# Attention and soft mixture of experts on one core: in blocks 2 and 3 the subtraction of k on GpSimd goes in halves behind the subtraction of q, and ScalarE casts q ahead of k

## The chip, the cores and the metric

The kernel runs on one core of one Trainium2 chip. The time is that of one execution on the device in microseconds (us), measured over several runs; a profile is one further execution, with a record of every instruction. TensorE (PE, with its weight loads shown as PEld), VectorE (DVE), ScalarE (ACT) and GpSimd (POOL) compute; the sync engine's queue (SP) issues nearly all the transfers.

## The reference, cut to what matters

```python
# q, k, v: (8, 12, 448, 64)
scores = 0.125 * q @ k.T            # causal mask, each of 96 heads
attn = exp(scores - rowmax) / (rowsum + 1e-9)
x = (attn @ v) as (3584, 768)
logits = x @ phi                    # phi: (768, 32)
slot_input = softmax_over_tokens(logits).T @ x
slot_out = per expert: relu(slot_input @ w1[e]) @ w2[e]     # 8 experts, 768 -> 1024 -> 768
out = softmax_over_slots(logits) @ slot_out
```

All arrays are float32.

## The kernel before, in words

The 96 heads are taken as 48 pairs, and `block(p)` works on pair p: heads a = 2p and a + 1. It is a software pipeline written out by hand, and each engine keeps the program's order. While block p finishes the softmax of pair p and multiplies by v, it already computes the first part of the scores of pair p + 1 (heads a + 2 and a + 3), subtracts for pairs p + 1 and p + 2, casts q of pair p + 2 and k of pair p + 3, and loads pairs p + 3 and p + 4. So "block 2" and "block 3" are the third and fourth pair.

The products are formed from float32 split in two: a rounded part in the type fp32r, and the rest.

- `cast_k` and `cast_q` (ScalarE) round raw k and q into the tiles `ks` and `qd`. There are two `ks` tiles, used by pairs in turn, but one `qd`.
- `sub_k` and `sub_q` (GpSimd, `TENSOR_TENSOR`) write the rests: that of k into the lower half of `ks`, that of q into the lower half of `r2`. A pair has 2 x 448 columns, and `slice(0, 1)` and `slice(1, 2)`, called h0 and h1, are its two heads. `sub_q` of the next pair has to wait until the matmuls of `scores2` have read the old `r2`, and `cast_q` has to wait until `sub_q` has read the old `qd`.
- `scores1_all(i)` (TensorE) adds the mask and multiplies `ks` by `qd` for head i. It is named s<-qd,ks in the profile; its first weight load has 66 columns.
- `max_keys`, `max_row` (VectorE and a transpose on TensorE) find maxima of blocks of queries: the small tile `mr`, one for each head.
- `max_spread(i)` (GpSimd, `AFFINE_SELECT`) spreads `mr` of head i into the upper rows of `r2`, as 14 x 448.
- `scores2(i)` (TensorE, s<-r,k in the profile) multiplies `r2` by a second copy of rounded k, `k2`, on top of the first scores: it adds the product with the rest of q and takes off the maximum. It needs both `sub_q` and the spread.
- `exps` (ScalarE, pt<-s) takes the exponential, and `attv_pair` (TensorE, po<-va,pt) multiplies by v. `norm`, `xtrans` and `xcopy` bring the result into x; in blocks with p odd, `logits_a` adds 8 calls of four small products to TensorE.

In block p, TensorE runs `scores2(a)`, `scores1_all(a + 2)`, `scores2(a + 1)`, `scores1_all(a + 3)`, `attv_pair(p)`, a transpose for `max_row`, in some blocks logits, `xtrans`. GpSimd runs, in blocks from 2 on, `sub_k(p + 2)`, `sub_q(p + 1)`, spread of head a + 2, spread of head a + 3. Block 1 has its own order there: q of head 0, k of head 0, q of head 1, two spreads, then k of head 1 at the block's end.

A load is issued on SP behind the subtraction that frees its buffer: `load_qk(p + 4, 1)` (raw k) behind `sub_k(p + 2)`, `load_qk(p + 3, 0)` (raw q) behind `sub_q(p + 1)`. There are two raw buffers each. SP is one queue and keeps its order, so a load that waits holds those behind it.

All engine calls go through one helper, so the profile gives them all line 67; they are told apart by tiles.

Of the kernel before, what the change touches and what calls it, by code (L numbers as in the profile page):

```python
# [82 lines left out]
def attention_soft_moe(ctx: ExitStack, tc: tile.TileContext, qk, va, phi, w, out):  # L83
# [43 lines left out]
    def load_qk(p, a, hs=slice(0, 2), eng=nc.sync):  # L127
        if p < NPAIR:
            if hs.start == 0:

                st["raw", a, p] = (qk0[:, WN * 2 * a:WN * 2 * a + 2 * S].rearrange("p (h s) -> p h s", h=2)
                                   if (p, a) in ((1, 0), (2, 1)) else
                                   kraw[p % 2 if p > 1 else 1 - p] if a else qraw[p % 2 if p else 1])
            eng.dma_start(out=st["raw", a, p][:, hs], in_=qk[p, :, a, hs])

    def loads_v(p, eng=nc.sync):
        if p < NPAIR:
            eng.dma_start(out=va_[p % 2], in_=va[p])
# [30 lines left out]
    def load_w(n):  # L169
        if n < len(order):  # L170
            t = wtiles[order[n]] = slot(n, f"w{n}")
            q, g, c = place(n), (n + 2) // 4, WN * ((n + 2) % 4)
            if n < RES or n == NBUF or q >= RES + LATE2:
                nc.sync.dma_start(out=t, in_=w[g, :, c:c + WN])
            elif 4 <= q < RES and n > NBUF:
                if q % 4 == 3:
                    nc.sync.dma_start(out=group(n), in_=w[g])
            elif n % 2:
                t = group(n)
                nc.sync.dma_start(out=t[:, 2 * WN:] if q < RES else t, in_=w[g, :, c - WN:c + WN])  # L180
# [51 lines left out]
    def kv(p):  # L232
        return heads(ks_[p % NR])[:, :, 0:S]

    def cast_q(p, hs=slice(0, 2)):
        if p < NPAIR:
            nc.scalar.activation(out=qd[:, hs], in_=st["raw", 0, p][:, hs], func=AF.Copy)

    def cast_k(p, hs=slice(0, 2)):
        if p < NPAIR:  # L240
            nc.scalar.activation(out=kv(p)[:, hs], in_=st["raw", 1, p][:, hs], func=AF.Copy)

    def sub_k(p, hs=slice(0, 2), eng=None):
        if p < NPAIR:
            ks = kv(p)[64:P, hs]
            (eng or nc.gpsimd).tensor_tensor(out=ks, in0=st["raw", 1, p][64:P, hs], in1=ks, op=ALU.subtract)
# [6 lines left out]
    def sub_q(p, hs=slice(0, 2), eng=None):  # L253
        if p < NPAIR:
            (eng or nc.gpsimd).tensor_tensor(out=r2[64:P, hs], in0=st["raw", 0, p][64:P, hs],
                                             in1=qd[64:P, hs], op=ALU.subtract)
# [67 lines left out]
    def max_spread(i):  # L324
        if i >= NHD:
            return
        p, h = divmod(i, 2)
        mr = st.pop(("mr", i))

        nc.gpsimd.affine_select(out=r2[0:NQB, h].rearrange("p (b t)->p b t", t=32),  # L330
                                in_=mr.unsqueeze(1).to_broadcast([NQB, NQB, 32]),
                                compare_op=ALU.is_equal, fill=0.0, base=0,
                                pattern=[[-1, NQB], [0, 32]], channel_multiplier=1)

    def scores2(i, cs):
        if i >= NHD:
            return
        p, h = divmod(i, 2)
        s = st["s", i]
        k2 = k2_  # L340
        for c in cs:
            o, w, m = KS * h + P * c, S - CQ0[c], min(P, KS - P * c)
            nc.tensor.matmul(s[0:m, SCOL[c]:SCOL[c] + w], k2[:, o:o + m],
                             r2[:, h, CQ0[c]:S], start=False, stop=True, skip_group_check=True)
# [60 lines left out]
    def norm(p, k):  # L405
        if k == 0:
            sm = st["sm", p] = moe.tile([P, NQ], F32, tag="sm", name=f"sm{p}", bufs=2)
            nc.vector.tensor_scalar(out=sm, in0=po2[:, :, HD], scalar1=EPS, scalar2=None, op0=ALU.add)
        elif k == 1:
            nc.vector.reciprocal(out=st["sm", p], in_=st["sm", p])  # L410
        else:
            x, sm = x_of(p), st.pop(("sm", p))
            m = NCH - 1
            nc.vector.tensor_tensor(out=x[:, 0:m].rearrange("p c (h d)->p h c d", h=2),
                                    in0=po2[:, 0:2 * m, 0:HD].rearrange("p (h c) d->p h c d", h=2),
                                    in1=sm[:, 0:2 * m].rearrange("p (h c)->p h c", h=2).unsqueeze(3)
                                    .to_broadcast([P, 2, m, HD]), op=ALU.mult)
            for h in range(2):
                a = AW * h
                nc.vector.tensor_scalar(out=x[0:AW, m, HD * h:HD * h + HD], in0=po2[a:a + AW, 2 * m, 0:HD],  # L420
                                        scalar1=sm[a:a + AW, 2 * m:2 * m + 1], scalar2=None, op0=ALU.mult)
# [95 lines left out]
    h0, h1 = slice(0, 1), slice(1, 2)  # L517
# [52 lines left out]
    def block(p):  # L570
        a, b = 2 * p, p // 6 - 1
        m6 = p % 6
        if p + 1 < NPAIR:
            loads_v(p + 1, nc.sync if p + 1 < NPAIR - 1 else nc.scalar)
        if p % 2 and p < 44 or p in (16, 30):
            load_w(st["w"])
            st["w"] += 1

        if p:
            norm(p - 1, 2)  # L580
        scores2(a, range(NCH))
        exps(a)
        if p == 0:
            copy_k2(0, h1)
            cast_q(1, h1)
            warm(START[3], pob)
            max_row(1, 0)
            max_row(1, 1)
            max_spread(1)
            sub_k(1, h1, nc.vector)  # L590
        elif p > 1:
            xcopy(p - 2)
        scores1_all(a + 2)
        if p == 0:
            warm(START[2], pob)
        for k in range(3):
            max_keys(a + 2, k)
        if p == 0:
            cast_k(2, h0)
        scores2(a + 1, range(NCH))  # L600
        exps(a + 1)
        if p == 0:
            cast_k(2, h1)
        scores1_all(a + 3)
        if m6 == 2 and p > 6:
            logits_b(b)
        max_keys(a + 3, 0)
        late_k = p == 1
        if p == 1:
            sub_q(2, h0)  # L610
            sub_k(3, h0)
            sub_q(2, h1)
            load_qk(4, 0)
        elif p:
            sub_k(p + 2, h0 if late_k else slice(0, 2))
            if not late_k:
                load_qk(p + 4, 1)
            sub_q(p + 1)
            load_qk(p + 3, 0)
        else:  # L620
            sub_q(1, h0)
            sub_q(1, h1)
            load_qk(3, 0)
            sub_k(2, h0)
        copy_k2(p + 1)
        if m6 == 2 and p > 6:
            logits_d(b, lt)
        if p:
            cast_k(p + 3)
            cast_q(p + 2)  # L630
        else:
            cast_q(2)
            cast_k(3)
        if m6 == 3 and p > 6:
            logits_al(b)
        elif m6 == 4 and p > 6:
            logits_n(b)
        attv_pair(p)
        max_row(a + 2, 1)
        max_spread(a + 2)  # L640
        if p == 0:
            sub_k(2, h1)
            load_qk(4, 1)
        for k in (1, 2):
            max_keys(a + 3, k)
        for k in range(2):
            norm(p, k)

        m = s_[(a + 1) % 3]
        parts = []  # L650
        if m6 in (1, 3, 5) and p > 1:
            j = (m6 + 3) % 6
            logits_a(b if m6 == 1 else p // 6, (j, j + 1), m[:, 0:P])
        elif m6 == 2 and p > 6:
            logits_e(b, m, 0)
        if m6 == 3 and p > 6:
            parts = [(b, 0, slice(0, P), 512)]
        elif m6 == 4 and p > 6:
            parts = [(b, 0, slice(P, 3 * P), 512)]
        elif m6 == 0 and p > 6:  # L660
            parts = [(b - 1, 1, slice(0, 3 * P), 0)]
        for d, hf, sl, o in parts:
            dispatch_a(d, hf, m[:, o:o + sl.stop - sl.start], sl)
        max_row(a + 3, 0, to=m[:, 1024 - P:1024])
        max_row(a + 3, 1)
        if m6 == 2 and p > 6:
            logits_e(b, m, 1)
        max_spread(a + 3)
        if late_k:
            sub_k(p + 2, h1)  # L670
            load_qk(p + 4, 1)
        if m6 in (1, 3, 5) and p > 1:
            logits_t(j, m[:, 0:P])
        for d, hf, sl, o in parts:
            dispatch_b(d, hf, m[:, o:o + sl.stop - sl.start], sl)
        if p:
            xtrans(p - 1)
# [8 lines left out]
    i, b, p = NHD - 1, NB - 1, NPAIR - 1  # L686
# [319 lines left out]
```

## Time and profile before

| what | before |
|---|---|
| median of three runs | 396.44 us (396.0 to 397.08) |
| the profiled execution, its own time | 395.86 us |
| its span, first to last instruction | 394.1 us |
| mean granted TensorE clock | 0.987 |
| PE busy | 365.4 us (93%) |
| PEld busy | 293.3 us (74%) |
| DVE busy | 294.9 us (75%) |
| ACT busy | 283.0 us (72%) |
| POOL busy | 256.6 us (65%) |
| load of raw k, 448 KB, median from issue to landing | 4.3 us |

The busy shares are means over the whole span. In the timeline rows used below the columns are the start in us from the span's start, the duration in us, the engine, the source line, the operation, the tile written and the tiles read, the shapes and the count; in square brackets stands the engine's idle time before the row and what ended it. In the chain of waits, which follows the last instruction back to what released it, the columns are start, duration and what.

### The profile page before, as it was taken

The numbers are of one execution on the slowest core, as the hardware profiler recorded it, in microseconds if no ns is written. First come the engines' busy times: TensorE is split into PE (matmuls) and PEld (weight loads), VectorE is DVE, ScalarE is ACT, GpSimd is POOL, SyncE is SP. The second block draws the span as 40 slices with busy tenths as digits, with TensorE's granted clock in tenths as the row PEclk, the third lists the DMA queues.
The fourth block names the chain that finished last, engine by engine and source line by source line (L and its number), as shares of the span: only waits on it lengthen the run. The fifth ranks groups of instructions, "written<-read, shape, count | busy, mean of one in ns | idle before, by whom it ended". The sixth has DMA issues, their size and how long they took to land.

```text
span 394.1 us, 14000 instructions
## 1 busy us (share of the span) xinstructions
PE 365.4 (93%) x5766; PEld 293.3 (74%) x5766; DVE 294.9 (75%) x835; ACT 283.0 (72%) x397; POOL 256.6 (65%) x214
## 2 busy tenths in 40 slices
PE   7899999999999999999999999999999998997840
PEld 3689889888988998898889888988986544533420
DVE  7787889888888888898888988888885575433540
ACT  5888889888898898888988989888864011432430
POOL 5998889888898888898988988889861000000000
PEclk9999999999999999999999999999999999999995
DMA  7858887778898788787987876887579999999997
GB/s 259 306 194 283 293 285 247 254 256 276 286 312 275 239 276 284 254 248 266 318 308 235 307 238 244 279 283 258 176 250 374 414 438 425 429 423 415 430 433 324
DMA packets 28720, 119.17 MB, mean 302 GB/s; under 512 B 3440, under 2 KB 3952, under 8 KB 26480
## 3 DMA queue, kind: packets, MB, share of 16 engines
q1 hardware_dynamic: 28512, 118.01, 82.9%
q8 instruction: 45, 0.74, 0.7%
q10 hardware_dynamic: 144, 0.27, 0.2%
q14 instruction: 19, 0.16, 0.1%
HBM read 107.25 MB, written 11.01 MB: 300 GB/s over the span
## 4 chain that ended last, share of the span: by engine, by line
PE 64%; DMA 11%; POOL 9%; DVE 6%; ACT 4%; issue 2%; SPq 0%; POOLq 0%; DVEq 0%; ACTq 0%
PE s L67 35%; PE po L67 20%; DMA w<-in_w_dram 9%; POOL r L67 6%; PE xm L67 4%; POOL ks L67 3%; DVE lm L67 2%; PE rt L67 2%; DMA kraw<-in_qk_dram 2%; DVE lg L67 1%; ACT qd L67 1%; PE pp L67 1%; PE e L67 1%; DVE si L67 1%; ACT w L67 1%
## 5 line engine op out<-in xcount | busy, mean ns | idle before, releaser
L67 DVE TRANSPOSE_TENSOR_REDUCE r<-s 128x32 f32<-128x1024 f32 x96 | 119.5, 1245 | 7.4 <-PE s L67 4.7
L67 ACT ACTIVATE pt<-s 128x1024 f32<-128x1024 f32 x96 | 98.7, 1029 | 30.8 <-PE s L67 22.5
L67 PEld LDWEIGHTS po<-va,pt 128*64 128x64 f32 x3040 | 103.6, 138 | 12.0 <-issue 11.5
L67 PE MATMUL po<-va,pt 128*64 128x65 f32 x3040 | 110.6, 224 | 0.0
L67 POOL TENSOR_TENSOR r<-qraw,qd 64x896 fp32r<-64x896 f32 (+1 forms) x49 | 99.3, 2027 | 3.2 <-ACT qd L67 1.8
L67 POOL TENSOR_TENSOR ks<-kraw,ks 64x896 fp32r<-64x896 f32 (+1 forms) x48 | 89.7, 1870 | 4.1 <-ACT ks L67 0.4
L67 POOL TENSOR_SCALAR_AFFINE_SELECT r<-mr 14x448 fp32r<-14x448 f32 x96 | 61.8, 644 | 31.9 <-DVE mr L67 27.2
L67 PE MATMUL s<-qd,ks 128*66 128x64 f32 (+3 forms) x384 | 80.2, 320 | 0.0
L67 PE MATMUL s<-r,k 128*128 128x448 f32 (+3 forms) x384 | 65.1, 291 | 3.1 <-POOL r L67 3.1
L67 PEld LDWEIGHTS s<-r,k 128*128 128x128 f32 (+1 forms) x384 | 59.3, 175 | 8.8 <-POOL r L67 6.6
L67 PEld LDWEIGHTS s<-qd,ks 128*128 128x128 f32 (+1 forms) x384 | 52.1, 182 | 2.0 <-issue 0.9
L67 ACT ACTIVATE ks<-kraw 128x896 fp32r<-128x896 f32 (+1 forms) x49 | 45.0, 920 | 5.3 <-DMA kraw<-in_qk_dram 4.1
L67 ACT ACTIVATE k<-ks 64x896 fp32r<-64x896 f32 (+1 forms) x49 | 45.8, 935 | 1.2
L67 ACT ACTIVATE qd<-qraw 128x896 fp32r<-128x896 f32 (+1 forms) x48 | 44.7, 931 | 1.3 <-POOL r L67 0.7
L67 PE MATMUL s<-tri,identb 128*128 128x192 bf16 x192 | 39.2, 268 | 0.6
L67 DVE TENSOR_REDUCE r<-r 128x16 f32<-128x32 f32 x192 | 33.7, 176 | 5.0
L67 DVE TENSOR_REDUCE mr<-s 14x32 f32<-14x128 f32 x47 | 13.1, 279 | 21.9 <-ACT qd L67 14.1
L67 PE MATMUL xm<-ident,x 128*128 128x128 f32 x188 | 28.3, 273 | 0.0
L67 ACT ACTIVATE xts<-xm 128x512 f32<-128x512 f32 x46 | 27.1, 590 | 0.0
L67 DVE TENSOR_SCALAR x<-po,sm 64x64 f32<-64x64 f32 x94 | 26.0, 276 | 0.7
L67 DVE TENSOR_TENSOR x<-po,sm 128x384 f32<-128x384 f32 x47 | 25.2, 537 | 0.0
L67 DVE COPY w<-pp 128x384 f32<-128x384 f32 x28 | 14.4, 553 | 13.2 <-PE pp L67 13.1
(148 smaller groups left out, 393.6 us busy)
## 6 DMA issues: line engine op xcount, KB each, us to landing
w<-in_w_dram SPq DMA_DIRECT2D x34, 768.0 KB, 6.6
kraw<-in_qk_dram SPq DMA_DIRECT2D x46, 448.0 KB, 4.3
qraw<-in_qk_dram SPq DMA_DIRECT2D x46, 448.0 KB, 4.5
w<-in_w_dram SPq DMA_DIRECT2D x5, 3072.0 KB, 23.9
va<-in_va_dram SPq DMA_DIRECT2D x47, 260.0 KB, 4.9
out_dram<-w SPq DMA_DIRECT2D x7, 1536.0 KB, 13.3
w<-in_w_dram SPq DMA_DIRECT2D x5, 1536.0 KB, 9.9
qk<-in_qk_dram SPq DMA_DIRECT2D x2, 448.0 KB, 7.2
```

The costliest lines, as they stand in the source:

```text
L67: return self._tc.keep_in_program_order(op(*args, **kwargs))
```

## The change

Three places of `block(p)` change, for p = 2 and p = 3 alone. GpSimd takes the whole subtraction of q first, then the spread of head a + 2, then k of head 0, the spread of head a + 3, and k of head 1. ScalarE casts q ahead of k. The loads move with the subtractions behind which they stand.

```diff
-        late_k = p == 1
         if p == 1:
             sub_q(2, h0)
             sub_k(3, h0)
             sub_q(2, h1)
             load_qk(4, 0)
+        elif p in (2, 3):
+            sub_q(p + 1)
+            load_qk(p + 3, 0)
         elif p:
-            sub_k(p + 2, h0 if late_k else slice(0, 2))
-            if not late_k:
-                load_qk(p + 4, 1)
+            sub_k(p + 2)
+            load_qk(p + 4, 1)
             sub_q(p + 1)
             load_qk(p + 3, 0)
...
-        if p:
+        if p in (2, 3):
+            cast_q(p + 2)
+            cast_k(p + 3)
+        elif p:
             cast_k(p + 3)
             cast_q(p + 2)
...
         max_spread(a + 2)
+        if p in (2, 3):
+            sub_k(p + 2, h0)
...
         max_spread(a + 3)
-        if late_k:
+        if 1 <= p <= 3:
             sub_k(p + 2, h1)
             load_qk(p + 4, 1)
```

GpSimd, from the last subtraction of block 1 into block 4, before. `mr6` to `mr11` are the maxima of heads 6 to 11; `ks0` holds pairs 4 and 6, `ks1` pairs 3 and 5.

```order
L67 TENSOR_TENSOR ks1_87<-kraw1_83,ks1_87 64x448
L67 TENSOR_TENSOR ks0_85<-kraw0_82,ks0_85 64x2x448
L67 TENSOR_TENSOR r2_93<-qraw1_88,qd_86 64x896
L67 AFFINE_SELECT r2_93<-mr6_474 14x448
L67 AFFINE_SELECT r2_93<-mr7_483 14x448
L67 TENSOR_TENSOR ks1_87<-kraw1_83,ks1_87 64x2x448
L67 TENSOR_TENSOR r2_93<-qraw0_84,qd_86 64x896
L67 AFFINE_SELECT r2_93<-mr8_565 14x448
L67 AFFINE_SELECT r2_93<-mr9_582 14x448
L67 TENSOR_TENSOR ks0_85<-kraw0_82,ks0_85 64x2x448
L67 TENSOR_TENSOR r2_93<-qraw1_88,qd_86 64x896
L67 AFFINE_SELECT r2_93<-mr10_664 14x448
```

Now, from the first instruction of block 2 (behind the same `ks1` half) to the subtraction of q in block 4:

```order
L67 TENSOR_TENSOR r2_93<-qraw1_88,qd_86 64x896
L67 AFFINE_SELECT r2_93<-mr6_472 14x448
L67 TENSOR_TENSOR ks0_85<-kraw0_82,ks0_85 64x448
L67 AFFINE_SELECT r2_93<-mr7_482 14x448
L67 TENSOR_TENSOR ks0_85<-kraw0_82,ks0_85 64x448
L67 TENSOR_TENSOR r2_93<-qraw0_84,qd_86 64x896
L67 AFFINE_SELECT r2_93<-mr8_564 14x448
L67 TENSOR_TENSOR ks1_87<-kraw1_83,ks1_87 64x448
L67 AFFINE_SELECT r2_93<-mr9_582 14x448
L67 TENSOR_TENSOR ks1_87<-kraw1_83,ks1_87 64x448
L67 TENSOR_TENSOR ks0_85<-kraw0_82,ks0_85 64x2x448
L67 TENSOR_TENSOR r2_93<-qraw1_88,qd_86 64x896
```

The whole subtraction of k in front of each block has become two halves, one on each side of the second spread; block 4 has its old order again, and its whole subtraction of k stands right behind the last half of block 3.

ScalarE in blocks 3 and 4, before and now, from the copy into `k2` in block 3 to the two casts of block 4 (`pt` are the exponentials, `xts` the copy of x):

```order
L67 ACTIVATE k2_92<-ks0_85 64x2x448
L67 ACTIVATE ks0_85<-kraw0_82 128x2x448
L67 ACTIVATE qd_86<-qraw1_88 128x896
L67 ACTIVATE pt0_94<-s2_81 128x1024
L67 ACTIVATE xts2_600<-xm2_586 128x512
L67 ACTIVATE pt1_95<-s0_79 128x1024
L67 ACTIVATE k2_92<-ks1_87 64x2x448
L67 ACTIVATE ks1_87<-kraw1_83 128x2x448
L67 ACTIVATE qd_86<-qraw0_84 128x896
```

```order
L67 ACTIVATE k2_92<-ks0_85 64x2x448
L67 ACTIVATE qd_86<-qraw1_88 128x896
L67 ACTIVATE ks0_85<-kraw0_82 128x2x448
L67 ACTIVATE pt0_94<-s2_81 128x1024
L67 ACTIVATE xts2_602<-xm2_588 128x512
L67 ACTIVATE pt1_95<-s0_79 128x1024
L67 ACTIVATE k2_92<-ks1_87 64x2x448
L67 ACTIVATE ks1_87<-kraw1_83 128x2x448
L67 ACTIVATE qd_86<-qraw0_84 128x896
```

The casts have changed places in block 3 (and likewise in block 2), while in block 4 k is still cast ahead of q.

SP, the loads of blocks 2 to 4, before and now (`kraw0` and `kraw1` here are raw k of pairs 6 and 7, then 8; `qraw1` and `qraw0` raw q of pairs 5 and 6):

```order
L67 DMA kraw0_82<-in_qk_dram 128x896
L67 DMA qraw1_88<-in_qk_dram 128x896
L67 DMA va0_89<-in_va_dram 128x520
L67 DMA w0_310<-in_w_dram 128x1536
L67 DMA kraw1_83<-in_qk_dram 128x896
L67 DMA qraw0_84<-in_qk_dram 128x896
L67 DMA va1_96<-in_va_dram 128x520
L67 DMA kraw0_82<-in_qk_dram 128x896
```

```order
L67 DMA qraw1_88<-in_qk_dram 128x896
L67 DMA kraw0_82<-in_qk_dram 128x896
L67 DMA va0_89<-in_va_dram 128x520
L67 DMA w0_310<-in_w_dram 128x1536
L67 DMA qraw0_84<-in_qk_dram 128x896
L67 DMA kraw1_83<-in_qk_dram 128x896
L67 DMA va1_96<-in_va_dram 128x520
L67 DMA kraw0_82<-in_qk_dram 128x896
```

In both blocks raw q is loaded ahead of raw k, and raw k waits for the second half of its subtraction.

## The prediction

> **What bounds the kernel now.** I read the chain of waits first. In the early blocks it runs over GpSimd, and it ends in the stream of weights behind the attention part (start, duration, what):
>
> ```profile
> 24.58 1.90 POOL ks L67
> 26.48 1.93 POOL r L67
> ...
> 332.03 35.70 DMA w<-in_w_dram
> ```
>
> The place of the change is therefore on the path that sets the end, and the question is only how much earlier or later TensorE leaves it. The second view is the timeline of weight loads on TensorE in blocks 2 to 4. Block 3 starts at 29.30 with `scores2` of head 6, block 5 at 41.04 with that of head 10:
>
> ```profile
> 27.66 0.47 PEld L67 LDWEIGHTS xm<-ident,x 128*128 128x128 f32 x4
> 29.30 0.60 PEld L67 LDWEIGHTS s<-r,k 128*128 128x128 f32 x4 [1.17 <-POOL r L67]
> ...
> 29.88 0.15 PEld L67 LDWEIGHTS s<-qd,ks 128*66 128x66 f32 x1
> ...
> 31.15 0.14 PEld L67 LDWEIGHTS s<-qd,ks 128*66 128x66 f32 x1
> ...
> 31.95 0.78 PEld L67 LDWEIGHTS po<-va,pt 128*64 128x64 f32 x24 [0.25 <-issue]
> ...
> 41.04 0.60 PEld L67 LDWEIGHTS s<-r,k 128*128 128x128 f32 x4 [0.44 <-POOL r L67]
> ```
>
> TensorE waits 1.17 us for the spread of head 6 and 0.44 us for that of head 10. These are the two waits the edit can touch. The third view is GpSimd over the same stretch:
>
> ```profile
> 23.61 2.88 POOL L67 TENSOR_TENSOR ks<-kraw,ks 64x448 fp32r<-64x448 f32 x2
> 26.43 2.10 POOL L67 TENSOR_TENSOR r<-qraw,qd 64x896 fp32r<-64x896 f32 x1
> 28.60 1.25 POOL L67 TENSOR_SCALAR_AFFINE_SELECT r<-mr 14x448 fp32r<-14x448 f32 x2
> 29.93 1.94 POOL L67 TENSOR_TENSOR ks<-kraw,ks 64x896 fp32r<-64x896 f32 x1
> 31.83 2.11 POOL L67 TENSOR_TENSOR r<-qraw,qd 64x896 fp32r<-64x896 f32 x1
> 34.01 0.64 POOL L67 TENSOR_SCALAR_AFFINE_SELECT r<-mr 14x448 fp32r<-14x448 f32 x1
> 35.54 0.64 POOL L67 TENSOR_SCALAR_AFFINE_SELECT r<-mr 14x448 fp32r<-14x448 f32 x1 [0.90 <-DVE mr L67]
> 36.26 1.94 POOL L67 TENSOR_TENSOR ks<-kraw,ks 64x896 fp32r<-64x896 f32 x1
> 38.17 2.10 POOL L67 TENSOR_TENSOR r<-qraw,qd 64x896 fp32r<-64x896 f32 x1
> 40.34 1.25 POOL L67 TENSOR_SCALAR_AFFINE_SELECT r<-mr 14x448 fp32r<-14x448 f32 x2
> ```
>
> From 23.61 to 41.6 GpSimd stands still once (gaps under 0.1 us aside), for 0.90 us, waiting for the maxima of head 9. Everywhere else it goes from one instruction to the next. So in these blocks it is GpSimd's amount of work that sets the pace, and changing its order can win no more than that 0.90 us, less whatever new idle time and new work it brings.
>
> **The change, part by part.** I follow GpSimd through the new order. Its gaps are read from the rows above: 0.07 us from a subtraction to a spread (33.94 to 34.01), 0.08 us from a spread to a subtraction, 1.91 us from start to start behind a whole k (36.26 to 38.17), and 0.06 us from the end of a spread (28.60 + 0.64 = 29.24) to TensorE's load at 29.30. A half of k has two prices, from the groups of GpSimd by shape around 19.6 (head 0 of pair 3) and around 23.6 us (head 1 of the same pair):
>
> ```profile
> L67 POOL TENSOR_TENSOR ks<-kraw,ks 64x448 fp32r<-64x448 f32 x1 | 1.2, 1151 | 0.0
> L67 POOL TENSOR_TENSOR ks<-kraw,ks 64x448 fp32r<-64x448 f32 x1 | 1.0, 975 | 0.1
> ```
>
> I take 1.15 for the first half and 0.975 for the second: 2.13 us instead of 1.94, so 0.19 more in each of the two blocks. The lower bound is 0.975 for each. [...]
>
> The maxima come from VectorE, in these rows:
>
> ```profile
> 26.87 0.24 DVE L67 TENSOR_REDUCE mr<-rt 14x32 f32<-14x128 f32 x1
> ...
> 32.39 1.24 DVE L67 TRANSPOSE_TENSOR_REDUCE r<-s 128x32 f32<-128x1024 f32 x1
> 33.55 0.24 DVE L67 TENSOR_REDUCE mr<-rt 14x32 f32<-14x128 f32 x1
> ...
> 35.20 0.28 DVE L67 TENSOR_REDUCE mr<-s 14x32 f32<-14x128 f32 x1 [0.51 <-PE s L67]
> ```
>
> *Block 2.* The half from block 1 ends at 23.61 + 0.975 = 24.59. The whole q starts there and ends at 26.69, 1.84 earlier than before (28.53). The spread of head 6 now waits for VectorE: 26.87 + 0.24 + 0.06 = 27.17, so GpSimd idles 0.4 us that it did not idle before; it ends at 27.81. First half of k: 27.89 to 29.04. Spread of head 7: 29.11 to 29.75. Second half: 29.83 to 30.80.
>
> *Block 3 on TensorE.* `scores2` of head 6 may start when the transposes end, 27.66 + 0.47 = 28.13: the 1.17 us are gone. But `scores1` now wants each half of k as it comes. Head 8 would load 0.58 later, at 28.71, and its half is there at 29.10; head 9 stood at 31.15, could have stood at 29.98 and gets its half at 30.80 + 0.06 = 30.86. Of the 1.17 us gained, 0.29 are left. ScalarE's exchange has to be counted here: with k cast first, as before, q of pair 4 would be ready only at the old 29.88, 0.78 after 29.10. The exchange alone brings nothing, since the halves of k would come too late as well, but the new order needs it. Its cover is that the old `qd` is read by 26.69.
>
> *Block 3 on GpSimd.* The q of pair 4 runs from 30.80 to 32.90. The maxima of head 8 lag the load at 31.15 by 2.40, of which I take 0.33 as a queue on VectorE that the stalls of TensorE now empty (bound: nothing of it): 30.86 + 2.07 = 32.93, done at 33.17. Spread of head 8: 33.23 to 33.87. First half of k: 33.95 to 35.10. The maxima of head 9 end 35.48 before, 0.29 earlier now, at 35.19; spread: 35.25 to 35.89, against 35.54 to 36.18. Second half: 35.97 to 36.95. And only then comes block 4's k, at 36.95 instead of 36.26.
>
> *Block 4.* Its order is the old one: k until 38.86, q until 40.96, spread of head 10 from 41.03 to 41.67, and `scores2` at 41.73 instead of 41.04. TensorE, ready at about 40.3 to 40.6 (41.04 - 0.44 = 40.60 before), waits longer than it did: **+0.69 us**. The early 1.17 us is a wait moved from the start of block 3 to the start of block 5, where 0.975 us of k stand in its way that in the old order were done before the spread.
>
> *The loads.* Raw k of pair 7 is now issued behind the second half, at 36.95 + 0.05 = 37.0 us; before it was at 31.89. ScalarE casts it in block 4, ahead of q:
>
> ```profile
> 39.44 0.95 ACT L67 ACTIVATE ks<-kraw 128x896 fp32r<-128x896 f32 x1
> 40.30 0.96 ACT L67 ACTIVATE qd<-qraw 128x896 fp32r<-128x896 f32 x1
> ```
>
> From the start of the k cast to the end of q's are 41.26 - 39.44 = 1.82 us, and the q is what `scores1` of head 12 waits for in block 5. How long the load takes has to come from the loads of the same size. The SP rows, and the landings of the k loads issued at 31.89 and at 38.23:
>
> ```profile
> 29.41 0.42 SPq L67 DMA_DIRECT2D w<-in_w_dram  x1
> 31.89 0.33 SPq L67 DMA_DIRECT2D kraw<-in_qk_dram  x1
> ...
> 38.23 0.33 SPq L67 DMA_DIRECT2D kraw<-in_qk_dram  x1
> ```
>
> ```profile
> kraw<-in_qk_dram SPq DMA_DIRECT2D x1, 448.0 KB, 5.8
> kraw<-in_qk_dram SPq DMA_DIRECT2D x1, 448.0 KB, 3.6
> ```
>
> The first stood 2.5 us behind a load of weights. The new place is 5 to 6 us behind that load (it goes out behind raw k of pair 6, after 30.85) and is nearer to the second, so I take 3.6, with 5.8 as the far bound. Landing 40.6, q cast until 42.42, load on TensorE at 42.48. By GpSimd alone it would be at 41.73 + 0.58 = 42.31; before it was at 41.04 + 0.58 = 41.62. The sum is 42.48 - 41.62 = **+0.86 us**, 0.69 from GpSimd and 0.17 from the load. [...]
>
> Raw k of pair 6 goes from 26.51 (behind its whole subtraction) to 30.85 and lands at 34.5 to 36.7; cast 0.95, it is ready at 35.4 to 37.6, and GpSimd wants it at 36.95. At 3.6 us it costs nothing, since the spreads and the second half of k cover it; at 5.8 it costs 0.7. The v and the weights behind it on SP start some 2 us later, and v is read in block 4's product, about 6 us on. The q loads start earlier and gate nothing.
>
> Behind block 5 the two programs are the same, and the chain ends in loads that start only when the attention part is done, so I carry the shift to the end unchanged. The profiled execution, 395.86 us of its own, would become 396.7. The median of the runs is 0.58 above it: 396.44 + 0.86 = **397.3 us**.
>
> **The rivals.** (1) *The gain is kept.* If GpSimd were not the pace of block 4, TensorE would keep the 1.17 us, and without block 5's wait 0.44 more: 395.3 to 394.8. For it speaks that 1.17 is by far the longest wait and that the edit surely removes it. Against it, GpSimd has no idle time but 0.90 us, and spends 0.4 and 0.3 on new waits. Even with halves at 0.975 and no stall of `scores1`, the spread of head 9 could not start before about 34.7, and the rest, 0.64 + 0.08 + 0.975 + 1.91 + 2.17 + 0.64 + 0.06, sets block 5 to 41.2. (2) *No difference.* That cheap end is it: +0.1 to +0.3, 396.6. (3) *Clearly slower.* The late load of raw k of pair 7 decides. It exceeds my sum by each tenth that it takes over 3.6 us, and passes +1.19 at 3.95 us. At 5.8 it sets `scores1` of head 12 to 44.68: +3.1, 399.5; at a middling 4.5, +1.8, 398.2. For it speaks that the fast row had an emptier queue than this one may find; against it, that weights go out 5 us before. That the edit doesn't do what it says is excluded by the listed order.
>
> **How the numbers follow.** The forecast (+0.5 to +1.19) has 0.48, the neutral case 0.19, the late load 0.26, the kept gain 0.07. About 0.3% (1.19 us) is what a measurement of this kernel tells from no change. Faster by more: 0.05, the rest of the kept gain counts as same; within: 0.69; slower: 0.26. The likeliest's own range is 396.9 to 397.6. The range to 8 in 10 takes in the neutral case and the middling late load: 395.8 to 398.4.
>
> **What would show it.** In the changed profile: `scores2` of head 6 at 28.1 to 28.2 without a wait; weight loads of heads 8 and 9 in block 3 that wait for GpSimd's ks, near 29.1 and 30.9; the k of block 4 starting at 36.9 rather than 36.26; `scores2` of head 10 at 41.7 behind a wait of over 1 us; ScalarE idle for the load of raw k before 40.6. If GpSimd begins block 4's k before 36.26, the sum is wrong and there is a gain; if raw k of pair 7 lands after 40.95, the change is slower by more than can be missed.

## The result: half a per cent slower

| | before | after |
|---|---|---|
| median of six runs | 396.44 us (396.0 to 397.08) | 398.3 us (397.89 to 399.71) |
| the profiled execution, its own time | 395.86 us | 397.89 us |
| its span | 394.1 us | 396.2 us |
| mean granted TensorE clock | 0.987 | 0.984 |

The ratio is 1.0052, with an interval of 1.0041 to 1.0063: some 2 us more, where the forecast was 0.86 us more, which is within what such a measurement tells from no change. Taken again beside other kernels, the change gave 398.46 us in seven runs and 1.0053 (1.0033 to 1.0073).

The order did on GpSimd what its rows said. The timeline of GpSimd after the change, from the q of block 2 to the spread of head 10:

```profile
24.64 2.09 POOL L67 TENSOR_TENSOR r<-qraw,qd 64x896 fp32r<-64x896 f32 x1
27.13 0.64 POOL L67 TENSOR_SCALAR_AFFINE_SELECT r<-mr 14x448 fp32r<-14x448 f32 x1 [0.40 <-DVE mr L67]
27.85 1.15 POOL L67 TENSOR_TENSOR ks<-kraw,ks 64x448 fp32r<-64x448 f32 x1
...
29.79 0.98 POOL L67 TENSOR_TENSOR ks<-kraw,ks 64x448 fp32r<-64x448 f32 x1
...
35.91 0.98 POOL L67 TENSOR_TENSOR ks<-kraw,ks 64x448 fp32r<-64x448 f32 x1
37.38 1.92 POOL L67 TENSOR_TENSOR ks<-kraw,ks 64x896 fp32r<-64x896 f32 x1 [0.50 <-ACT ks L67]
...
41.43 1.24 POOL L67 TENSOR_SCALAR_AFFINE_SELECT r<-mr 14x448 fp32r<-14x448 f32 x2
```

Down to the last half at 35.91 every start lies within 0.1 us of the predicted one. Then block 4's k waits 0.50 us, and not for GpSimd's own work: for ScalarE's cast. ScalarE says why:

```profile
36.30 0.95 ACT L67 ACTIVATE ks<-kraw 128x896 fp32r<-128x896 f32 x1 [2.48 <-DMA kraw<-in_qk_dram]
37.16 1.00 ACT L67 ACTIVATE pt<-s 128x1024 f32<-128x1024 f32 x1
...
41.11 0.95 ACT L67 ACTIVATE ks<-kraw 128x896 fp32r<-128x896 f32 x1 [0.57 <-DMA kraw<-in_qk_dram]
```

It stands idle for 2.48 us until the raw k of pair 6 is there, and behind the cast stand the exponentials of head 8, at 37.16 instead of 36.00. A block later it waits again, for the raw k of pair 7. On TensorE, in the timeline of weight loads:

```profile
28.05 0.60 PEld L67 LDWEIGHTS s<-r,k 128*128 128x128 f32 x4
29.05 0.13 PEld L67 LDWEIGHTS s<-qd,ks 128*66 128x66 f32 x1 [0.32 <-POOL ks L67]
...
30.82 0.14 PEld L67 LDWEIGHTS s<-qd,ks 128*66 128x66 f32 x1 [0.38 <-POOL ks L67]
...
38.22 0.14 PEld L67 LDWEIGHTS s<-qd,ks 128*66 128x66 f32 x1 [1.50 <-issue]
...
42.12 0.59 PEld L67 LDWEIGHTS s<-r,k 128*128 128x128 f32 x4 [0.38 <-POOL r L67]
42.96 0.14 PEld L67 LDWEIGHTS s<-qd,ks 128*66 128x66 f32 x1 [0.17 <-ACT qd L67]
```

The 1.17 us ahead of head 6 are gone, as predicted, and heads 8 and 9 wait for the halves of k at 29.05 and 30.82. But head 11 stalls by 1.50 us (its load is at 38.22, before at 37.08). The row of weight loads names no cause; that of head 11's first product on TensorE does:

```profile
38.21 0.24 PE L67 MATMUL s<-tri,identb 128*128 128x192 bf16 x1 [1.43 <-ACT pt L67]
```

It writes into the scores that the late exponentials still read. Block 5's `scores2` stands at 42.12 and head 12 at 42.96, against 41.04 and 41.62 before. The chain of waits of the changed kernel runs through the load:

```profile
29.79 0.99 POOL ks L67
30.79 5.42 DMA kraw<-in_qk_dram
...
36.30 0.96 ACT ks L67
...
37.41 1.89 POOL ks L67
39.31 2.06 POOL r L67
```

From the second half of k, to the load that it sets free, to the cast, to GpSimd's next k. The load took 5.42 us.

To compare executions I use the transposes of x that end each block on TensorE (xm<-ident,x). The first 20 us scatter by up to 0.8 us between executions of any kernel here, so the end of block 1 is taken off as the start. The shift against the profiled execution of before is then, at the end of block 5 (46.52 us before):

| kernel | end of block 1 | end of block 5 | shift |
|---|---|---|---|
| before | 22.12 | 46.52 | 0 |
| after | 22.07 | 47.76 | +1.29 |
| both raw k loaded early | 22.77 | 47.78 | +0.61 |
| raw k of pair 6 early | 22.16 | 47.72 | +1.16 |
| raw k of pair 7 early | 22.88 | 48.62 | +1.34 |
| after, second profile | 22.58 | 49.90 | +2.92 |

Of the 2.03 us between the two profiled executions 1.2 are there by block 5 and stay until the attention part ends. The rest comes behind it, where both kernels run the same code: the wait for the weights, 35.70 us of the chain before, is 36.06 after, and the writing of the output adds the remainder. In that part single executions scatter (the profiled one with both raw k loaded early loses nothing there), so I draw nothing from it.

### The profile page after: what moved, and what is told of

The parts are those of the page before. It is cut to its first block, busy times and chain, and to the rows that moved or that the text cites. A ratio compares the mean times of both kernels' runs of the same rounds, so it can differ in the third digit from the quotient of the medians.

```text
span 396.2 us, 14004 instructions
## 1 busy us (share of the span) xinstructions
PE 365.8 (92%) x5766; PEld 293.5 (74%) x5766; DVE 295.1 (75%) x835; ACT 282.8 (71%) x397; POOL 256.8 (65%) x216
## 4 chain that ended last, share of the span: by engine, by line
PE 61%; DMA 10%; DVE 9%; POOL 7%; ACT 6%; issue 3%; POOLq 0%; ACTq 0%; DVEq 0%
PE s L67 33%; PE po L67 19%; DMA w<-in_w_dram 9%; POOL r L67 4%; PE xm L67 4%; POOL ks L67 3%; DVE lm L67 2%; PE rt L67 2%; ACT qd L67 1%; DMA kraw<-in_qk_dram 1%; DVE r L67 1%; DVE lg L67 1%; DVE si L67 1%; PE pp L67 1%; PE e L67 1%
```

## The experiments

### Both late loads taken away, GpSimd's order kept

```diff
-                                   if (p, a) in ((1, 0), (2, 1)) else
+                o = {(1, 0): 0, (2, 1): 2 * WN, (6, 1): 2 * WN, (7, 1): 0}.get((p, a))
...
         elif p in (2, 3):
+            load_qk(p + 4, 1)
             sub_q(p + 1)
...
             sub_k(p + 2, h1)
-            load_qk(p + 4, 1)
+            if p == 1:
+                load_qk(p + 4, 1)
```

> The changed kernel, but raw k of pairs 6 and 7 gets memory of its own (the place of two early tiles that are no longer used), so its loads go out near where they stood before the change, and GpSimd's new order is all that is left of the change. Theory A (two costs: GpSimd's order by itself, and on top of it the late loads of raw k): block 4's k on GpSimd starts at 36.9 without a wait for ScalarE, scores2 of head 10 loads at 41.7, scores1 of head 12 at 42.3; from block 5 on TensorE is 0.7 us behind the kernel before instead of 1.25, and the time is 0.6 us below that of the changed kernel. Rival B (the late loads alone make the loss, GpSimd's new order costs nothing): scores1 of head 12 at 41.6, time as before.

Measured: 397.26 us beside 396.6 of before, 1.001 (1.0001 to 1.0019). TensorE's and GpSimd's timelines of this kernel (two fences, GpSimd first):

```profile
36.61 0.98 POOL L67 TENSOR_TENSOR ks<-kraw,ks 64x448 fp32r<-64x448 f32 x1
37.55 1.95 POOL L67 TENSOR_TENSOR ks<-qk,ks 64x896 fp32r<-64x896 f32 x1
```

```profile
37.64 0.13 PEld L67 LDWEIGHTS s<-qd,ks 128*66 128x66 f32 x1 [0.21 <-POOL ks L67]
42.31 0.59 PEld L67 LDWEIGHTS s<-r,k 128*128 128x128 f32 x4 [1.17 <-POOL r L67]
```

GpSimd goes from the half to block 4's k without a wait, head 11 waits only 0.21 us, for its half of k, and the loss stands in one wait of 1.17 us for the spread of head 10 (0.44 before): the wait that the change removes ahead of head 6 has come back there, as 0.7 us more than before. The shift is +0.61, the median +0.66. That is the predicted 0.69 us of GpSimd alone. The loads make the rest, some 1.2 us of the median.

### Each load by itself

The same edit for one of the two pairs only, the other load staying behind its half (shown for pair 6; for pair 7 it is the entry `(7, 1): 0`, and 3 in place of 2):

```diff
+                o = {(1, 0): 0, (2, 1): 2 * WN, (6, 1): 2 * WN}.get((p, a))
...
+            if p == 2:
+                load_qk(p + 4, 1)
...
-            load_qk(p + 4, 1)
+            if p != 2:
+                load_qk(p + 4, 1)
```

> The change, with raw k of pair 6 alone loaded early (into free memory of an early tile); raw k of pair 7 still waits for the second half of its subtraction, at 36.9 us. Theory A (the two late loads act side by side: that of pair 6 holds GpSimd's subtraction, the exponentials and head 11, that of pair 7 holds the casts of block 4 and head 12, and the later of the two counts): ScalarE's wait in block 4 for raw k of pair 6 is gone and head 11 doesn't stall, but scores1 of head 12 still stands at 42.9 behind the cast of q (landing 41.0, casts 1.82, 0.06), so the shift of block 5 stays +1.2 to +1.3 and only the long executions disappear: 397.6 to 398.0 us, +1.1 to +1.4 over before, no execution at a mean clock of 0.975 in which block 4's product runs at half speed. Theory B (pair 6's load is the whole excess): the shift falls to GpSimd's +0.62 and the time to that with both loads early, +0.65 over before, about 397.2.

> The change, with raw k of pair 7 alone loaded early; raw k of pair 6 still waits for the second half of its subtraction, at 30.8 us. Theory A (two loads side by side): block 4's k on GpSimd still waits for the cast of pair 6, head 11 still stalls by 1 to 2 us, scores2 of head 10 stands at about 42.1 and scores1 of head 12 at 42.7, a shift of +1.1; 397.8 to 398.4 us, +1.2 to +1.9 over before, and some executions at a mean clock of 0.975 that are 1.5 to 2 us longer. Theory B (pair 6 alone): nothing changes against the change itself, +1.7 to +2.0, 398.3. Theory C (pair 7's load alone, which the prediction's rival named): the time falls to +0.65 over before, 397.2.

Measured: pair 6 early 397.63 us, 1.0023 (1.0015 to 1.0032); pair 7 early 397.78 us, 1.0025 (1.0015 to 1.0036); before 396.57 beside them. With pair 6 early, TensorE has its long wait for GpSimd again, and then one more, for ScalarE, which waited for pair 7 (ScalarE, then TensorE):

```profile
41.07 0.95 ACT L67 ACTIVATE ks<-kraw 128x896 fp32r<-128x896 f32 x1 [1.91 <-DMA kraw<-in_qk_dram]
```

```profile
41.70 0.59 PEld L67 LDWEIGHTS s<-r,k 128*128 128x128 f32 x4 [1.15 <-POOL r L67]
42.91 0.13 PEld L67 LDWEIGHTS s<-qd,ks 128*66 128x66 f32 x1 [0.55 <-ACT qd L67]
```

With pair 7 early, pair 6 alone does the same damage by the other way (ScalarE, GpSimd, TensorE):

```profile
37.32 0.95 ACT L67 ACTIVATE ks<-kraw 128x896 fp32r<-128x896 f32 x1 [2.70 <-DMA kraw<-in_qk_dram]
```

```profile
38.40 1.92 POOL L67 TENSOR_TENSOR ks<-kraw,ks 64x896 fp32r<-64x896 f32 x1 [0.71 <-ACT ks L67]
```

```profile
39.23 0.14 PEld L67 LDWEIGHTS s<-qd,ks 128*66 128x66 f32 x1 [1.71 <-issue]
```

The shifts, +1.16 and +1.34, are those of the change itself (+1.29). They are also what the rows add up to: 0.61 for GpSimd's order and 0.55 for ScalarE's q make 1.16 with pair 6 early, 0.61 and GpSimd's 0.71 make 1.32 with pair 7 early. So the two loads act side by side, and the later of the two paths counts. Taking away one buys almost nothing in a profile. By the profiles the theory that pair 6 is the whole excess (397.2 with it early) falls, and so does the one that pair 7 is (397.2). The times alone would hardly decide: 397.2 is a ratio of 1.0016, just inside both intervals. In the medians, each against before beside it, either gains 0.65 to 0.8 us on the change (1.06 and 1.21 over before, against 1.86). Part of that is scatter of the landings, and part the next point.

### The change again, and a half clock

> The changed kernel once more, beside the kernel before on the same chip. In the first profile TensorE was 1.25 us behind from block 5 on and the span 2.1 us longer, so 0.9 us lay behind block 5. Theory S (that rest is the scatter of start and weight stream from one execution to the next): the time is 1.2 to 1.6 us above before, and in this profile raw k of pairs 6 and 7 land at another delay than 5.4 and 4.2 us, with TensorE's lag following them between 0.65 and 1.3 us. Rival (the rest belongs to the change): 1.9 us or more above before again, with the lag at the end larger than at block 5.

Measured: 398.46 us, 1.85 over the 396.61 of before beside it. That lies between the 1.2 to 1.6 of theory S and the 1.9 of its rival, and decides for neither. The profile of this execution (399.84 us) is of the longer kind. Raw k of pair 6 landed 6.07 us after its issue, and TensorE's weight loads read:

```profile
39.38 0.14 PEld L67 LDWEIGHTS s<-qd,ks 128*66 128x66 f32 x1 [2.14 <-issue]
...
40.20 1.38 PEld L67 LDWEIGHTS po<-va,pt 128*64 128x64 f32 x24 [0.29 <-issue]
...
41.57 2.30 PEld L67 LDWEIGHTS po<-va,pt 128*64 128x64 f32 x39
```

Before, the same two groups took 0.78 and 1.40 us. The table of stretches (after the busy times: granted clock, share of the DMA engines, GB/s) shows TensorE idle for the whole of one microsecond and then at half its clock, for 3.4 us (0.46 + 0.50 + 0.50 + 0.24 of a microsecond missing, over 0.5; the stretch from 41 to 42 is left out here and has 0.50):

```profile
38.00:39.00 1.00, 0.00 (x0) 0.00 (x0) 0.49 (x3) 1.00 (x2) 0.45 (x1) 1.00 0.68 151
39.00:40.00 1.00, 0.62 (x6) 0.54 (x5) 0.00 (x0) 1.00 (x3) 1.00 (x1) 1.00 0.87 336
40.00:41.00 1.00, 1.00 (x16) 0.80 (x16) 0.62 (x1) 0.98 (x2) 1.00 (x2) 0.54 0.87 328
...
42.00:43.00 1.00, 1.00 (x23) 1.00 (x23) 0.55 (x3) 0.76 (x1) 0.86 (x2) 0.50 0.82 314
43.00:44.00 1.00, 1.00 (x23) 0.93 (x20) 0.00 (x0) 1.00 (x2) 0.30 (x1) 0.76 0.65 156
```

The shift of this execution is +2.92, 1.63 more than in the first profile and above the 0.65 to 1.3 that theory S allowed; a part of that is the later landing, not the clock. It stays as it is to the end of the attention part, so it does not grow behind block 5, as the rival would have it. Of the 13 executions of the change, four have a mean clock of 0.975 and times of 399.5 to 400.25; the other nine lie at 0.98 to 0.986 and 397.34 to 398.7, with a median of 398.07. That all four had the half clock in block 4 is argued from the clock; one was profiled. None of the executions with one or both loads early is at 0.975 (0.979 and over, 30 of them), also not the eight with pair 7 alone early, where some were expected.

### A longer stall, to see whether it brings the half clock

```diff
             sub_k(p + 2, h1)
-            load_qk(p + 4, 1)
+            if p != 2:
+                load_qk(p + 4, 1)
...
         if p % 2 and p < 44 or p in (16, 30):
             load_w(st["w"])
             st["w"] += 1
+        if p == 3:
+            load_qk(6, 1)
```

> The change, with the load of raw k of pair 6 moved on SP behind the v and the weights of block 3, so that it is issued at about 32.1 instead of 30.8 us and lands at 37 to 38.5; TensorE's stall before head 11 grows from 1.4 to between 2.2 and 3.7 us. Theory G (a stall of TensorE of about 2 us, as in the second execution of the change where it was 2.07, makes the granted clock fall to 0.5 for some 3.4 us, in which block 4's product takes about twice its time): the profile shows the clock at 0.5 behind the stall, weight loads of the first 24 of that product in 1.1 to 1.4 us instead of 0.78, a mean clock at or under 0.976 in nearly all executions, and a time of 400.5 to 402 us, +4 to +5.5 over before. Rival H (the half clock in that execution had nothing to do with the stall): the stall alone is added, 1.0 to 2.3 us over the change's undisturbed executions (398.0), so 399.0 to 400.3, with the clock at 1.0 behind it and a mean clock of 0.98 and more.

Measured: 398.43 us, 1.0051 (1.0038 to 1.0064), in four runs. The load was not issued later than in the change: v and the weights, which it now stands behind, wait for nothing and went out ahead of it. But it took longer, in the chain of waits:

```profile
30.79 6.28 DMA kraw<-in_qk_dram
```

The stall ahead of head 11 grew, and the clock stayed up (TensorE's loads, then the stretches, 1.00 behind the busy times being the clock):

```profile
39.07 0.14 PEld L67 LDWEIGHTS s<-qd,ks 128*66 128x66 f32 x1 [2.35 <-issue]
...
39.87 0.78 PEld L67 LDWEIGHTS po<-va,pt 128*64 128x64 f32 x24 [0.26 <-issue]
```

```profile
40.00:42.00 2.00, 2.00 (x66) 2.00 (x65) 1.68 (x4) 1.89 (x3) 2.00 (x2) 1.00 0.49 137
```

Theory G, that a stall of about 2 us brings the half clock, fails in its plain form: behind a stall of 2.35 us the clock was 1.00 here, behind 2.14 it was 0.50 there, and one of these four executions (399.14) had a mean clock of 0.975. The shift, +2.00, is what the long load costs at full clock; against the +2.92 of the execution above, with a load of 6.07 us, the half clock is worth some 0.9 us, or 1.1 if the 0.2 us by which that load was shorter are counted. Rival H, that the stall had nothing to do with it, isn't shown either: every such low mean clock among these kernels belongs to one with a late raw k of pair 6 (0.975; all others are at 0.978 and over). When such a stall is followed by the half clock is not shown by these runs.

### ScalarE's exchange undone

```diff
-        if p in (2, 3):
-            cast_q(p + 2)
-            cast_k(p + 3)
-        elif p:
+        if p:
```

> The changed kernel with ScalarE's old order: k cast ahead of q in blocks 2 and 3 too. Theory A: q of pair 4 is ready only at about 29.8, so scores1 of head 8 loads near 29.8 instead of 29.05; worse, in block 3 q of pair 5 now stands behind the cast of the late raw k of pair 6 (landing 36.2), so scores1 of head 10 loads near 38.2 instead of 35.45 and block 5 starts near 43.0 instead of 42.1: 0.7 to 0.9 us slower than the changed kernel. Rival (the exchange of the casts is without effect, since GpSimd sets the pace): the time of the changed kernel within 0.3 us.

Measured: 398.25 us, 1.0037 (1.0023 to 1.0051); the expected 0.7 to 0.9 us over the change did not come. The wait that it was to bring is there. ScalarE's cast of q in block 2, and head 8 on TensorE behind it, at 30.25 instead of 29.05 (0.85 later with the start taken off):

```profile
29.21 0.93 ACT L67 ACTIVATE qd<-qraw 128x896 fp32r<-128x896 f32 x1
```

```profile
30.25 0.14 PEld L67 LDWEIGHTS s<-qd,ks 128*66 128x66 f32 x1 [1.17 <-POOL r L67]
```

But in this execution raw k of pair 6 landed in 3.50 us (issued at 31.15), and the shift at block 5 is +1.21, about that of the change. What block 3 loses here by the late q it did not lose by a long load. GpSimd shows the loss, in its subtraction of the q of pair 4, which follows without a wait in the change:

```profile
31.69 2.10 POOL L67 TENSOR_TENSOR r<-qraw,qd 64x896 fp32r<-64x896 f32 x1 [0.57 <-ACT xts L67]
```

The profile puts the wait down to a copy on ScalarE that the subtraction doesn't use. By the program it waits for `scores2` of head 7, which reads the old `r2`; its weights load here from 30.73 to 31.42, behind the late head 8. GpSimd's order, 0.61, and this 0.57 make 1.18 of the 1.21. So in this execution the old order of casts cost about 0.57 us, with a fast load. In the times, 398.25 against 398.3, the exchange's worth cannot be told from the scatter of the loads; a late load and a late q may well hide each other, which is not shown.

### What limits block 3 before the change

The prediction said that GpSimd's work sets the pace, and that the exchange alone brings nothing. Two kernels leave work out, a third moves it to VectorE:

```diff
-            sub_k(p + 2, h0 if late_k else slice(0, 2))
+            sub_k(p + 2, h0 if p == 2 else slice(0, 2))
```

> The kernel before, with head 1's half of the subtraction of k left out for pair 4 (the rest of k of that head stays as the cast left it, so its scores lack that correction): 0.975 us less work for GpSimd in block 2, nothing else. Rival C (GpSimd's amount of work alone sets the pace of blocks 2 to 4): the spread of head 6 0.8 to 0.97 us earlier, and TensorE 0.7 to 0.97 us ahead from block 3 on: time 0.7 to 0.9 us below before. Theory A with one more bound (in block 2 ScalarE casts k, which waits for its load until 28.0, ahead of q, so scores1 of head 8 cannot load before 29.88 anyway): scores2 of head 6 loads 0.7 earlier, scores1 of head 8 at 29.9 as before, and the time stays as before within 0.2 us.

Measured: 396.56 us, 0.9997 (0.9987 to 1.0007), no gain. The work gone from GpSimd, ScalarE's q takes its place; TensorE's loads of heads 6 and 8:

```profile
28.53 0.59 PEld L67 LDWEIGHTS s<-r,k 128*128 128x128 f32 x4 [0.36 <-POOL r L67]
...
30.04 0.13 PEld L67 LDWEIGHTS s<-qd,ks 128*66 128x66 f32 x1 [0.84 <-ACT qd L67]
```

The same with q cast ahead of k in block 2:

```diff
+        if p == 2:
+            cast_q(p + 2)
+            cast_k(p + 3)
+        elif p:
-        if p:
```

> The kernel before, with head 1's half of the subtraction of k of pair 4 left out, as in the run where this alone moved nothing, and now q cast ahead of k in block 2 as well. Theory A (GpSimd's work and the cast of q bound block 3 together): scores2 of head 6 at 28.55, scores1 of head 8 at 29.15 instead of 29.9, the spread of head 9 and with it block 4's k 0.5 to 0.7 us earlier, block 5 at 40.3 to 40.6 instead of 41.04: 0.4 to 0.7 us below before. Rival (neither sets the pace, the stretch is bound elsewhere, VectorE's reductions for instance): as before within 0.2 us.

Measured: 395.9 us, 0.9983 (0.9974 to 0.9991). TensorE loads head 8 at 29.85, which is 29.09 with the start taken off, instead of 29.88. So block 3 has two bounds that lie close together, GpSimd's sum of work and the cast of q behind the load of k: with GpSimd's alone eased nothing was gained, with both 0.7 us. Now the half is not left out but given to VectorE:

```diff
+        if p == 2:
+            sub_k(p + 2, h1, nc.vector)
         scores2(a, range(NCH))
```

> The kernel before, with two edits in block 2 alone: VectorE does head 1's half of the subtraction of k of pair 4, at the block's start (GpSimd does head 0's half and then goes on in the old order), and ScalarE casts q ahead of k. Theory A: both bounds of block 3's start are lifted together: spread of head 6 at 27.9 instead of 28.6, scores1 of head 8 near 29.15 instead of 29.88, block 4's k on GpSimd near 35.5 instead of 36.26, scores2 of head 10 near 40.3 instead of 41.04: 0.7 us below the kernel before. Rival (VectorE, which pays 0.7 us at 23.8, becomes the pace of block 2): maxima of heads 6 and 7 0.4 us later, and the time as before or up to 0.4 us above.

Measured: 396.59 us, 0.9996 (0.9988 to 1.0005), no gain. VectorE and GpSimd in this kernel, and behind them GpSimd's same two halves in the kernel with the half left out, and VectorE's two halves in the kernel before:

```profile
24.49 1.26 DVE L67 TENSOR_TENSOR ks<-kraw,ks 64x448 fp32r<-64x448 f32 x1
```

```profile
24.29 2.46 POOL L67 TENSOR_TENSOR ks<-kraw,ks 64x448 fp32r<-64x448 f32 x2
```

```profile
23.63 2.08 POOL L67 TENSOR_TENSOR ks<-kraw,ks 64x448 fp32r<-64x448 f32 x2
```

```profile
4.29 0.62 DVE L67 TENSOR_TENSOR ks<-kraw,ks 64x448 fp32r<-64x448 f32 x1
...
11.27 0.71 DVE L67 TENSOR_TENSOR ks<-kraw,ks 64x448 fp32r<-64x448 f32 x1
```

VectorE's half takes 1.26 us beside GpSimd's instead of 0.62 to 0.71, and GpSimd's two take 2.46 instead of 2.08. VectorE's maxima come behind it: those of head 6 are reduced at 28.54, 0.98 later than before with the start taken off (28.54 - 26.87 - 0.69). That eats most of the time won on GpSimd: the spread of head 6 starts at 28.87, right behind them, which is 0.4 us earlier than before with the start taken off, and not the expected 0.7. The shift at the end of block 5 is -0.27, too little to show in the time.

### A version that beats both

The run with both loads early says what to avoid: a load that hangs on the late half. And GpSimd stands idle in block 3, for 0.90 us, so one late half has room there. So: block 1's own order (half of k, q, two spreads, half of k) used in block 2 too, raw k of pairs 5 and 6 in free memory and loaded early:

```diff
+                o = {(1, 0): 0, (2, 1): 2 * WN, (5, 1): 0, (6, 1): 2 * WN}.get((p, a))
...
-        late_k = p == 1
+        late_k = p in (1, 2)
         if p == 1:
+            load_qk(5, 1)
...
-            if not late_k:
-                load_qk(p + 4, 1)
+            load_qk(p + 4, 1)
...
             sub_k(p + 2, h1)
-            load_qk(p + 4, 1)
```

> The kernel before, with GpSimd's order of block 1 in block 2 too (half of k, q, both spreads, the other half of k at the end), and raw k of pairs 5 and 6 in memory of their own, loaded early, so that nothing waits for a late load. Blocks 3 and later keep the old order. Theory A: the second half of k fills the 0.9 us in which GpSimd waits for the maxima of head 9, so the gain is real: scores2 of head 6 at 28.6 instead of 29.30, spread of head 9 at 35.0 instead of 35.54, block 5 at 40.5 instead of 41.04: 0.4 to 0.5 us below before. Rival (a gain in block 3 is lost to block 5 whatever the order, as in the changed kernel): as before, or up to 0.3 us above.

Measured: 395.86 us in twelve runs, 0.998 (0.9969 to 0.9991): 0.75 us faster than before (396.61) and 2.6 faster than the change (398.46), both beside it. Its shift at block 5 is -0.79, more than the expected 0.4 to 0.5. Both bounds are eased, by the rows of ScalarE's cast of k in block 2 (before it waited 1.24 us for the load) and of GpSimd's spreads in block 3 (before with the 0.90 us between them):

```profile
27.41 0.95 ACT L67 ACTIVATE ks<-qk 128x896 fp32r<-128x896 f32 x1
```

```profile
34.69 1.24 POOL L67 TENSOR_SCALAR_AFFINE_SELECT r<-mr 14x448 fp32r<-14x448 f32 x2
```

The early loads alone, without the order (late_k left at p == 1):

> The kernel before with the two early loads of the faster variant alone (raw k of pairs 5 and 6 in free memory, loaded early), and the order of GpSimd as before. Theory A (the faster variant gains by GpSimd's order in block 2, and the early loads are only what makes that order bearable): GpSimd's work still sets block 3, scores2 of head 6 waits about 1.2 us and stands at 29.3 plus the scatter of the start, and the time is that of before, 396.3 to 396.7 us (ratio 0.999 to 1.001). Rival L (the gain comes from the loads, which let ScalarE cast k and q earlier in block 2): 395.7 to 396.0, as the faster variant.

Measured: 396.52 us, 0.9999 (0.999 to 1.0009); TensorE waits as before:

```profile
30.04 0.60 PEld L67 LDWEIGHTS s<-r,k 128*128 128x128 f32 x4 [1.16 <-POOL r L67]
```

So the loads alone gain nothing; with the order they do. The order without the early loads was not tried; the kernel with the half left out, which gained nothing while q stood behind the load of k, speaks against it.

The same order in blocks 4 and 6 as well (late_k for p in 1, 2, 4, 6); in block 6 the early load of pair 10 overwrites raw k of pair 8 ahead of its second half, so the rest of k of one head is not the reference's there, with the amount of work unchanged (GpSimd doesn't wait for that load: the half starts at 54.00, 0.08 us behind the spread):

> The same with the late second half in blocks 2, 4 and 6. Theory A: block 5 at 40.4, block 7 at 52.1 instead of 52.77, and the half of block 6 pushes the q of block 7 so that 0.3 to 0.6 us are left from block 8 on. Rival: the raw k of pairs 8 and 10, whose buffers now come free only at the end of blocks 2 to 6, arrive late, and block 5 to 7 give the gain back: as before or slower.

Measured: 397.13 us, 1.0014 (1.0004 to 1.0023). Each further late half is paid for in the block behind it, where TensorE waits for the spread of heads 12 and 16:

```profile
47.61 0.59 PEld L67 LDWEIGHTS s<-r,k 128*128 128x128 f32 x4 [0.60 <-POOL r L67]
...
59.70 0.59 PEld L67 LDWEIGHTS s<-r,k 128*128 128x128 f32 x4 [0.59 <-POOL r L67]
```

The shift goes from -0.62 at the end of block 5 to +0.40 at that of block 8. GpSimd, which didn't rest in block 4 before, now stands idle there for 0.28, 0.40 and 0.46 us. This is the mechanism of the prediction, without any late load: k that has not been subtracted before the spreads stands ahead of the next block's k.

## Why the prediction was wrong, point by point

**GpSimd's part was right.** Spread of head 6 predicted at 27.17, found at 27.13; weight loads of heads 8 and 9 at 29.10 and 30.86, found at 29.05 and 30.82; spread of head 8 at 33.23, found at 33.25; last half at 35.97, found at 35.91; and +0.69 us for block 5 by GpSimd alone, +0.61 in the shift and +0.66 in the median with the loads taken out of the way. The price of a half, 1.15 and 0.975, was found as 1.15 and 0.98. That the wait ahead of head 6 would only move, to head 10, is shown.

**The step that failed is the landing of the two raw k loads, that of pair 6 above all**: "At 3.6 us it costs nothing" for pair 6 and "Landing 40.6" for pair 7. I took the faster of two rows for both, and weighed 5.8 for pair 6 in one clause. In the profile of the change pair 6 took 5.42 us and pair 7 4.1 (issued at 36.91, cast from 41.11). At the same place pair 6 took 3.50, 5.42, 5.63, 6.07 and 6.28 us in five executions of the change and its variants. Only one of the five is at 3.6 or under. Pair 7 took 3.3, 3.3, 3.9, 4.1 and 4.7 in five. So 3.6 lies within the range for pair 7, and at the bottom of it for pair 6, whose term, put at nothing, measured 0.50 us on GpSimd in the first profile and 0.71 to 1.35 in the three with a longer landing.

**By the prediction's own terms** pair 7 moved head 12 from the predicted 42.48 to 42.96: +1.34 instead of +0.86 (0.5 us of landing more makes +1.36 by the rule that I gave for it). The sign that I gave, a landing after 40.95, came true at 41.0. That is the rival "clearly slower", which named this load and its point, 3.95 us. The mechanism was written down; its chance, 0.26 against 0.48, was not earned by the rows, of which one of two spoke for it.

**What was missing** is the second path of pair 6's load. I had it hold back GpSimd only, at 0.7 for the far bound (0.50 was found). ScalarE keeps its order, so the exponentials of head 8 stand behind the waiting cast, and TensorE's head 11 behind them: a stall of 1.50 us which the sum did not contain. In the first profile it costs nothing, since TensorE waits for the spread of head 10 later anyway; in the second TensorE came out of it at half clock, some 0.9 us dearer. What starts the half clock stays open. The median over all 13 executions, 398.46, is some 0.4 us above that of the nine at 0.98 and over.

**Why removing one load was not enough** follows: the two paths join at block 5, one through GpSimd to head 10, one through ScalarE to head 12, and each is late by about as much.

**The rivals.** "The gain is kept" falls: with both loads early and GpSimd alone left, the change still loses 0.66 us. "No difference" falls by the interval, though that version comes near to it. The exchange of casts, costed at nothing alone, wasn't tried alone; but with half of k left out it makes the difference between 396.56 and 395.9. That GpSimd's work alone sets the pace was too strong: in block 3 the cast of q stands close behind it.

## What to carry to other kernels

When a subtraction moves, the load that waits for its buffer moves too; take its landing as a range that includes the slow rows, and ask for everything that the waiting engine has in its queue behind the consumer, not for the consumer alone. Where an engine never rests, changing its order only moves the wait, here 1.17 us from head 6 to head 10; it gains where the new order fills an idle stretch, as the single late half does (0.75 us). Two waits that join later must be removed together before either shows: one load early left shifts of +1.16 and +1.34, both early +0.61. Look at the clock behind a stall on TensorE as well: behind one of 2.14 us it was 0.50 for 3.4 us in one profile here, behind one of 2.35 it was 1.00 in another.

## What the runs showed of the hardware

- One 448 KB load, that of raw k of pair 6 behind the second half of its subtraction, took between 3.50 and 6.28 us from issue to landing in five executions of the change and its variants. No single row prices it.
- TensorE ran at a granted clock of 0.50 for 3.4 us behind a stall of 2.14 us in one execution, and at 1.00 behind one of 2.35 us in another. What decides is open.
- In the one profile in which VectorE and GpSimd subtract k side by side, VectorE's half took 1.26 us instead of 0.62 and 0.71 for its two halves in the kernel before, and GpSimd's two halves 2.46 instead of the 2.08 in the kernel with half of k left out. Why is not shown.
- Half of k took GpSimd 1.14 to 1.16 us for head 0 and 0.97 to 0.99 for head 1 in the profiles of the kernel before and of the change (both), and 1.14 to 1.15 and 0.98 in that with the late halves. Why the two differ is open.
